# Turning gathered rows of x in 32 by 32 squares on VectorE, from four part rows per token

## The chip, the core and the metric

The kernel runs on one core of one Trainium2 chip. The metric is the device time of one execution in microseconds. The core has TensorE (PE in the profile; PEld is its loading of weights), VectorE (DVE), ScalarE (ACT), GpSimd (POOL) and the queue engine SyncE (SP), which issues most DMAs. Each engine runs its own instructions strictly in order and waits on the others through semaphores. Three runs of the kernel before gave 692.34 to 692.62 us, with a median of 692.57 us.

## What is computed

A dilated sliding-window attention makes a token's features x (512 numbers: 8 heads of 64), and a mixture of experts with one expert per token turns them into the output. The second half is what matters here:

```python
logits = np.einsum('bsd,de->bse', x, w_gate)            # 8 x 576 tokens, 8 experts
local_gate = 1.0 / (1.0 + np.exp(-np.einsum('bsd,de->bse', x, w_local).squeeze(-1)))
for s in range(S):
    fresh_e = int(np.argmax(logits[b, s]))
    e = fresh_e if (s == 0 or local_gate[b, s] < 0.5) else prev_e
    prev_e = e
    h = np.maximum(x[b, s] @ w1[e], 0.0)                # 512 -> 1024
    out[b, s] = p[e] * (h @ w2[e])                      # 1024 -> 512, p: softmax of logits
```

All data are float32. Which tokens belong to which expert is known only on the chip, so tokens are grouped by expert there.

## The kernel before

**Attention and routing.** A loop over 32 head pairs (`for n in range(NPB + 2)`) makes scores, probabilities and values. Each finished group of two head pairs of one batch is written to a scratch tensor in DRAM by SP (`store`): `xd[0]` holds the 256 features of the plain heads of every token, `xd[1]` those of the dilated heads, whose tokens stand in another order. In the gaps of that loop, one step per call of `gap`, a list called `waiting` is worked off: it holds the routing of the four groups of two batches. After two groups `early_tokens` can name the tokens of the first two units; after all four, in the gaps of the expert stage, `late_tokens` names the rest. `tokens(late)` does it: one matrix product of `acc` (the positions of all tokens, as codes) with `chosen` gives `fp`, in which partition p and column c hold the code of the p-th token of tile c, and a few integer operations on VectorE make two row numbers from it, `tok` for `xd[0]` and `pos` for `xd[1]`.

**The expert stage** works on units. A unit is a `pair` (two tiles of 128 tokens of one expert), a `full` (one tile) or a `half` (64 tokens). Two pairs come early, units 0 and 1; 22 late units follow. Numbered from zero they are P P P F P H, then P P F P H, the same five again, P P F P, and P H at the end (P pair, F full, H half); the text calls them i0 to i21. So i3, i8, i13, i18 are full and i5, i10, i15, i21 are half. For a unit u:

- `gather(u)`: GpSimd fetches its rows by an indirect DMA, one for `tok` and one for `pos` per tile, 1 KB per row, into `xg` (two buffers).
- `features(u)`: TensorE turns each tile's 128x512 into four 128x128 blocks in a PSUM bank `tp` (L820), ScalarE copies them to `xe` (L821). For a pair, four VectorE operations then make the sums `xc` (L787 to L790).
- `hidden(u)`: the first layer. For a pair it is Strassen's scheme in Winograd's form (`chain`): seven products over quarters of the matrices, with sums of the weights (`sums[0]`, four VectorE operations of 128x1024) and of the features (`xc`). Three PSUM banks x, y, z take them in turn; the first, third, fifth and seventh product go into x. `keep` copies a product away on ScalarE, `finish` adds to it on VectorE (L910).
- `output(u)`: the second layer, the same with seven products and the sums `hc` of the hidden values and `sums[1]` of the weights; `finish` writes `y` on VectorE (L984), and `send` scatters `y` to the output from GpSimd, one indirect DMA per tile. A full ends with one VectorE operation on `y` (L960).

The loop over late units is the order in which TensorE and VectorE get their work, since for these two engines the order is that of the program:

```python
for u in range(FIRST, NU):
    run_hidden(u, both(u - 1) if u > FIRST else [])   # both: hc sums and sums[1] of unit u-1, on VectorE
    if u + 1 < NU:
        features(u + 1)
        if u + 2 < NU:
            gather(u + 2)
    push = sums_of_weights(u + 1, False) if is_pair(u + 1) else []   # sums[0] of unit u+1
    if u > FIRST:
        run_output(u - 1, push)
```

The sums that are pushed are spread over the gaps between products, and what is left is issued at the unit's end. GpSimd's, ScalarE's and SP's orders are made by a scheduler. For the first late unit, i0, `features` is called in the middle of the output of unit 1 (`feed`), and i0's hidden layer is followed at once by i1's, with no output between them.

## Time and profile before

| what | value |
|---|---|
| median of 3 runs | 692.57 us |
| the profiled execution | 695.8 us, its span 693.9 us |
| granted TensorE clock, mean | 0.981 |
| busy: PE, PEld, DVE, ACT, POOL | 95%, 84%, 58%, 28%, 27% |
| DMA | 131.40 MB, mean 189 GB/s |
| attention stage | to about 170 us |
| expert stage with early units | 170 to 233 us |
| late units | 233 to 680 us, then the last scatters |

A row of the table of groups gives line, engine, operation, what it writes and reads, how often, the busy time and the mean time of one. A row of the timeline gives the start in us, the time from the start of the first to the end of the last instruction that it merges, the engine, the line and the number of instructions; what stands in square brackets is the idle time of the engine before it and what ended it. A float32 product shows as two instructions, a TensorE transpose as one. Since matmuls overlap, the time that one takes from TensorE is read from start to start of neighbouring rows, not from its own length.

### The profile page before, as it was taken

To read this page: it belongs to the slowest core of one execution; us is meant where nothing else is said; L and a number is where in the kernel's file an instruction comes from. 1 tells how busy PE (TensorE), PEld (TensorE's weight loads), DVE (VectorE), ACT (ScalarE), POOL (GpSimd) and SP (SyncE) were. 2 spreads that over 40 slices of the span, in tenths; PEclk is the share of its full clock that TensorE was granted. 3 is DMA by queue.
4 is the path that set the end of the run, shared out by engine and by line. 5 is a ranking of instruction groups with operands and counts; after the bars stand their busy time and mean duration, and the time that the engine had idled before them with its cause. 6 is when DMAs were issued, how large, how long until landed. Compare 5 with 4: busy or idle time off the path is not lost. (4 is left out here: it accounts for less than half of the span.)

```text
span 693.9 us, 14608 instructions
## 1 busy us (share of the span) xinstructions
PE 661.4 (95%) x6102; PEld 581.9 (84%) x6102; DVE 401.2 (58%) x784; ACT 191.8 (28%) x350; POOL 184.0 (27%) x181
## 2 busy tenths in 40 slices
PE   8999898898998989999999999999999999999994
PEld 8878787786987989999599999599998799997973
DVE  3758697678767377363456472637451828446450
ACT  3544343342311232312223222123222132122310
POOL 4332212311012233122453141413241423041011
PEclk9999998998999999999999999999999999999998
DMA  9999776874502677565453414744113556451201
GB/s 351 409 376 329 265 245 227 275 277 129 215 30 83 236 317 298 224 220 224 146 198 137 153 54 152 278 177 156 31 40 123 210 184 247 145 194 30 113 32 42
DMA packets 27835, 131.40 MB, mean 189 GB/s; under 512 B 3981, under 2 KB 14349, under 8 KB 21744
## 3 DMA queue, kind: packets, MB, share of 16 engines
q1 hardware_dynamic: 20912, 110.97, 43.4%
q0 software_dynamic: 6848, 19.41, 7.9%
q8 instruction: 50, 0.82, 0.5%
q14 instruction: 25, 0.20, 0.1%
HBM read 145.04 MB, written 19.40 MB: 237 GB/s over the span
## 5 line engine op out<-in xcount | busy, mean ns | idle before, releaser
L928 POOL DMA_INDIRECT out_dram<-y,tok x36 | 49.7, 1380 | 250.8 <-DVE y L984 130.2
L969 PE MATMUL yp<-sum,hc 128*128 128x256 f32 x384 | 88.2, 379 | 0.0
L900 PE MATMUL hp<-xc,sum 128*128 128x128 f32 x720 | 85.6, 275 | 1.2 <-DVE sum L781 1.2
L910 DVE TENSOR_TENSOR h<-hp,h 128x512 f32<-128x512 f32 x45 | 30.9, 689 | 95.6 <-PE hp L900 95.3
L900 PEld LDWEIGHTS hp<-xc,sum 128*128 128x128 f32 x720 | 82.9, 192 | 1.4 <-DVE sum L781 1.4
L808 POOL DMA_INDIRECT xg<-xd,tok x40 | 47.1, 1178 | 131.2 <-PE tp L820 109.5
L969 PEld LDWEIGHTS yp<-sum,hc 128*128 128x128 f32 x384 | 72.8, 190 | 9.9
L984 DVE SCALAR_TENSOR_TENSOR y<-yp,gate,y 128x256 f32<-128x256 f32 x48 | 23.2, 482 | 69.2 <-issue 44.9
L317 ACT ACTIVATE pr<-pr 96x512 f32<-96x512 f32 x64 | 43.8, 684 | 67.3 <-DVE pr L314 64.3
L308 PE MATMUL sc<-kq 64*96 64x64 f32 x1152 | 56.5, 249 | 4.9 <-DVE pr L314 3.8
L314 DVE SCALAR_TENSOR_TENSOR pr<-sc,mk 96x512 f32<-96x512 f32 x64 | 46.8, 748 | 24.8 <-PE sc L308 22.6
L969 PE MATMUL yp<-raw,h 128*128 128x256 f32 x256 | 60.7, 380 | 0.0
L257 POOL COPY vt<-vt 32x585 f32<-32x585 f32 x48 | 33.9, 707 | 100.3 <-DMA vt<-in_v_dram 65.8
L308 PEld LDWEIGHTS sc<-kq 64*96 64x96 f32 x1152 | 52.2, 163 | 9.2 <-DVE pr L314 4.2
L900 PE MATMUL hp<-xe,raw 128*128 128x128 f32 x480 | 59.0, 276 | 0.3 <-ACT xe L821 0.3
L900 PEld LDWEIGHTS hp<-xe,raw 128*128 128x128 f32 x480 | 56.5, 192 | 2.9 <-issue 2.1
L969 PEld LDWEIGHTS yp<-raw,h 128*128 128x128 f32 x256 | 47.4, 190 | 6.7 <-issue 0.8
L362 PE MATMUL pv<-vt,pr 128*64 128x65 f32 x1152 | 44.6, 230 | 5.5 <-issue 5.0
L904 ACT COPY h<-hp 128x512 f32<-128x512 f32 x45 | 26.4, 586 | 77.6 <-PE hp L900 77.6
L362 PEld LDWEIGHTS pv<-vt,pr 128*64 128x64 f32 x1152 | 39.1, 143 | 9.7 <-issue 7.0
L808 POOL DMA_INDIRECT xg<-xd,pos x40 | 43.2, 1080 | 12.2 <-issue 12.2
L911 ACT ACTIVATE h<-h 128x512 f32<-128x512 f32 x45 | 28.3, 630 | 65.1 <-DVE h L910 63.5
(209 smaller groups left out, 990.3 us busy)
## 6 DMA issues: line engine op xcount, KB each, us to landing
raw<-in_w_dram SPq DMA_DIRECT2D x48, 2048.0 KB
kq<-in_qk_dram SPq DMA_DIRECT2D x15, 1184.0 KB
vt<-in_v_dram SPq DMA_DIRECT2D x15, 880.0 KB
xd<-x SPq DMA_DIRECT2D x16, 512.0 KB
kq<-in_qk_dram SPq DMA_DIRECT2D x2, 592.0 KB
xd<-x SPq DMA_DIRECT2D x32, 32.0 KB
xg<-xd,tok POOLq DMA_INDIRECT x40
xg<-xd,pos POOLq DMA_INDIRECT x40
```

The lines of the kernel that those rows point to most:

```text
L257: nc.gpsimd.tensor_copy(t[k * WIN:(k + 1) * WIN, VQ:], t[KW:, k * NB * VW:(k + 1) * NB * VW])
L308: nc.tensor.matmul(sc[:KW, u, (i - a) * QB:(i - a + 1) * QB], lhsT=kt[h, i * QB:i * QB + KW], rhs=qt[h, i * QB:(i + 1) * QB], start=True, ...
L314: nc.vector.scalar_tensor_tensor(to, sc[:KW, :, :w], -CEIL, mk[:, at:at + w].unsqueeze(1).to_broadcast([KW, 2, w]), Alu.max, Alu.min)
L317: nc.scalar.activation(to, to, Act.Exp, scale=SCALE)
L362: nc.tensor.matmul(pv[half * QB:(half + 1) * QB, k - a], lhsT=pr[:, u, (i - a) * QB:(i - a + 1) * QB], rhs=vt[:, u, i], start=True, stop=T ...
L808: nc.gpsimd.indirect_dma_start(out=x[:rows, g], out_offset=None, in_=xd[g] if units[u]["late"] else xd[g][:EARLY * GS], in_offset=bass.Ind ...
L900: nc.tensor.matmul(to[:, m], lhsT=a[:, m, kk], rhs=b[:, kk], start=first and m == 0 and kk == 0, stop=(kk == DK // 2 - 1), skip_group_chec ...
L904: nc.scalar.copy(at((0, 1, 3)[k]), of)
L910: nc.vector.tensor_tensor(at(k), of, at(k), op=Alu.add)
L911: nc.scalar.activation(at(k), at(k), Act.Relu)
L928: nc.gpsimd.indirect_dma_start(out=out, out_offset=bass.IndirectOffsetOnAxis(ap=of_unit(u, "tok", j), axis=0), in_=y, in_offset=None, boun ...
L969: nc.tensor.matmul(to, lhsT=a[:, m], rhs=b[:, m], start=first and m == 0, stop=(m == FK // 2 - 1), skip_group_check=True)
```

## The change

The scratch tensor becomes one tensor `xd` of [token][2][256], and is read as rows of 128 features (`xq`), four to a token. One indirect DMA now fetches, for 32 tokens, their four part rows of 512 bytes into four blocks of 32 partitions, so a tile of 128 tokens takes four of them (a half two) instead of two of 1 KB rows. VectorE then turns the tile in one operation in 32 by 32 squares, from `xg` straight to `xe`; TensorE's transposes and ScalarE's copies of the features are gone. The order of the features within a block of 128 is different, and the weights w1 are laid out to match on the host.

For the row numbers, `tokens` makes a second product `fq`: for each of the four groups of 32 tokens in a tile (`square`) four small products put the tokens' codes into the four blocks of partitions, 16 products for the early units and 32 for the late ones. Six VectorE operations over four times as many columns make the row numbers `at`; two operations that made `pos` are gone.

Gathers are called one unit further ahead, with four buffers for late units. `early_tokens` puts the second half of unit 0's gathers one step further down the list `waiting`, so every later step of that list comes one gap later.

```diff
-    xd = [dram.tile([N + 1, D // 2], F32, name=f"xd{g}") for g in range(2)]
+    xd = dram.tile([N + 1, 2, D // 2], F32, name="xd")
+    xq = xd.rearrange("n g (u f) -> (n g u) f", u=2)
...
         fp = bank([P, 2, cols], "fp")
+        fq = bank([P, NQS, cols], "fq")
         chosen = tiles["chosen", late]
+
+        def square(q, at, cols, first, flags):
+
+            for part in range(NQS):
+                nc.tensor.matmul(fq[part * SQ:(part + 1) * SQ, q, cols], lhsT=acc[:, at + q * SQ:at + (q + 1) * SQ],
+                                 rhs=of[:2 * ES, 0, cols], start=first, tile_position=(0, part * SQ), **flags)
+
...
+            if late:
+                nc.vector.tensor_copy(acc[:, P:], acc[:, ROW:P])
+            for q in range(NQS):
+                square(q, 0, slice(0, w), k == 0 and q == 0, flags)
+            if late:
+                for q in range(NQS):
+                    square(q, ROW, slice(C_HALF, cols), False, flags)
             nc.tensor.matmul(fp[:, :, :w], lhsT=acc[:, :P], rhs=of[:2 * ES, :, :w], start=(k == 0), **flags)
...
+        nc.vector.tensor_scalar(codes, fq, float(NONE), None, Alu.add)
+        nc.vector.tensor_scalar(high, codes, 8, None, Alu.logical_shift_right)
+        nc.vector.tensor_scalar(at, codes, 10, None, Alu.logical_shift_right)
+        nc.vector.tensor_scalar(high, high, a_high, a_part, Alu.mult, Alu.add)
+        nc.vector.scalar_tensor_tensor(high, at, a_batch, high, Alu.mult, Alu.add)
+        nc.vector.scalar_tensor_tensor(at, codes, a_code, high, Alu.mult, Alu.add)
...
-        nc.vector.scalar_tensor_tensor(base, c, float(CI - 1), base, Alu.mult, Alu.add)
-        nc.vector.tensor_tensor(pos, base, j, op=Alu.add)
...
-    def gather(u):
-        assert not xg
-        for j in range(2 if units[u]["kind"] == "pair" else 1):
-            rows = ROW if units[u]["kind"] == "half" else P
-            xg[u, j] = x = mw.tile([P, 2, D // 2], F32, name="xg")
-            for g, what in enumerate(("tok", "pos")):
+    def gather(u, only=None):
+
+        col, late = units[u]["col"], units[u]["late"]
+        for j, n in enumerate(tiles_of(u)):
+            if only not in (None, j):
+                continue
+            xg[u, j] = x = stage.tile([P, NQS, P], F32, name="xg", bufs=4) if late else mw.tile(
+                [P, NQS, P], F32, name="xg")
+            for q in range(n):
                 nc.gpsimd.indirect_dma_start(
-                    out=x[:rows, g], out_offset=None, in_=xd[g] if units[u]["late"] else xd[g][:EARLY * GS],
-                    in_offset=bass.IndirectOffsetOnAxis(ap=of_unit(u, what, j, rows), axis=0))
+                    out=x[:, q], out_offset=None, in_=xq if late else xq[:EARLY * GS * NQS],
+                    in_offset=bass.IndirectOffsetOnAxis(ap=tiles["at", late][:, q, col + j:col + j + 1], axis=0))
 
     def features(u):
-        kind = units[u]["kind"]
-        rows = ROW if kind == "half" else P
         xe[u] = mw.tile([P, DK, 2 * P], F32, name="xe")
-        for j in range(2 if kind == "pair" else 1):
-            x = xg.pop((u, j)).rearrange("p g f -> p (g f)")
-            tp = bank([P, DK, P], "tp")
-            for kk in range(DK):
-                nc.tensor.transpose(tp[:, kk, :rows], x[:rows, kk * P:(kk + 1) * P], ident[:rows, :rows])
-            nc.scalar.copy(xe[u][:, :, j * P:j * P + rows], tp[:, :, :rows])
+        for j, n in enumerate(tiles_of(u)):
+            x = xg.pop((u, j))[:, :n].rearrange("p q (k d) -> p k q d", k=DK)
+            nc.vector.transpose(xe[u][:, :, j * P:j * P + n * SQ].rearrange("p k (q t) -> p k q t", q=n), x)
...
     def early_tokens():
         tokens(False)
-        gather(0)
+        gather(0, 0)
+        waiting.insert(0, lambda: gather(0, 1))
 
     def late_tokens():
         tokens(True)
-        wanted.append(FIRST)
-        gather_wanted()
+        gather(FIRST)
+        gather(FIRST + 1)
...
         features(FIRST)
-        gather(FIRST + 1)
+        gather(FIRST + 2)
...
         if u + 1 < NU:
             features(u + 1)
-            if u + 2 < NU:
-                gather(u + 2)
+            if u + 3 < NU:
+                gather(u + 3)
```

**VectorE, the stretch from the end of a full's output to the output of the pair before the half.** Here `xe` and `xc` are those of the pair after a half (i6, i11, i16), `hc` and the first `sum` belong to the pair before it, and the second `sum` is `sums[0]` of the pair after it. Before, and with the change:

```order
L960 TENSOR_SCALAR y<-yp,gate_2902 128x512
L781 TENSOR_TENSOR hc<-h 128x512
...
L790 TENSOR_TENSOR sum_2536<-raw_0_79,sum_2536 128x1024
L787 TENSOR_TENSOR xc<-xe 128x256
...
L783 TENSOR_TENSOR sum_80<-raw_1_2531 128x1024
L984 SCALAR_TENSOR_TENSOR y<-yp,gate_2902,y 128x256
L784 TENSOR_TENSOR sum_80<-raw_1_2531,sum_80 128x1024
L984 SCALAR_TENSOR_TENSOR y<-yp,gate_2902,y 128x256 x2
```

```order
L856 STREAM_TRANSPOSE xe<-xg 128x4x64
L995 TENSOR_SCALAR y<-yp,gate_2954 128x512
L818 TENSOR_TENSOR hc<-h 128x512
...
L827 TENSOR_TENSOR sum_2555<-raw_0_78,sum_2555 128x1024
L856 STREAM_TRANSPOSE xe<-xg 128x4x128 x2
L824 TENSOR_TENSOR xc<-xe 128x256
...
L820 TENSOR_TENSOR sum_79<-raw_1_2550 128x1024
L1019 SCALAR_TENSOR_TENSOR y<-yp,gate_2954,y 128x256
L821 TENSOR_TENSOR sum_79<-raw_1_2550,sum_79 128x1024
L1019 SCALAR_TENSOR_TENSOR y<-yp,gate_2954,y 128x256 x2
```

Two transposes stand between the sums and `xc`, ahead of the two operations on `y` that release the banks; the half's own transpose stands ahead of the full's last operation.

**TensorE at the late tokens**, in the hidden layer of unit 1 (the products into `hp`). Before, and with the change:

```order
L665 MATMUL ep<-chosen_late,cst 1x48
L889 MATMUL hp<-xe,raw_1_2531 128x256 x4
L682 MATMUL fp<-chosen_late,acc 128x2x40
L685 MATMUL fp<-chosen_late,acc 128x2x8
L889 MATMUL hp<-xe,raw_1_2531 128x256 x8
L969 MATMUL yp<-raw_1_2537,h 128x256 x4
```

```order
L674 MATMUL ep<-chosen_late,cst 1x48
L924 MATMUL hp<-xe,raw_1_2550 128x256 x4
L688 MATMUL fq<-chosen_late,acc 32x40 x16
L688 MATMUL fq<-chosen_late,acc 32x8 x16
L706 MATMUL fp<-chosen_late,acc 128x2x40
L708 MATMUL fp<-chosen_late,acc 128x2x8
L924 MATMUL hp<-xe,raw_1_2550 128x256 x4
L1004 MATMUL yp<-raw_1_2556,h 128x256 x4
```

The 32 small products stand ahead of the two old ones, and four products of the hidden layer instead of eight are left behind them: the step comes one gap later.

**GpSimd from the first late gathers on** (`at_2934` are the late row numbers, `tok_2030` are the early units' and `tok_2947` the late ones' rows of the output). With the change:

```order
L848 DMA xg<-xd,at_2934 128x128 x24
L963 DMA out_dram<-y,tok_2030 4608x512 x2
L848 DMA xg<-xd,at_2934 128x128 x14
L963 DMA out_dram<-y,tok_2947 4608x512 x2
L848 DMA xg<-xd,at_2934 128x128 x4
```

The gathers of i0, i1 and i2 (24) stand ahead of unit 1's two scatters; before, it was the eight of i0 and i1.

48 lines of the change are left out of this document (30 added, 18 removed).

## The prediction

> **What bounds the kernel now.** I read the page's busy shares first, then who TensorE waited for, then the timeline around each `features`.
>
> ```profile
> PE 661.4 (95%) x6102; PEld 581.9 (84%) x6102; DVE 401.2 (58%) x784; ACT 191.8 (28%) x350; POOL 184.0 (27%) x181
> ```
>
> ```profile
> PE pv L362 <- issue: 5.0, 8, 1.1
> ...
> PE hp L900 <- DVE sum L781: 1.2, 1, 1.2
> ```
>
> Columns of the second view: total wait in us, times, longest. TensorE is busy 95% of the span, and its longest kind of wait (5.0 us in all) lies in attention. In the expert stage little stands in that view beside one wait of 1.2 us, at i1. So an instruction taken from TensorE there is worth its time, unless another engine is just behind. Whether VectorE is, tells this view:
>
> ```profile
> DVE xc L787 <- ACT xe L821: 27.7, 11, 3.0
> ```
>
> Of the 15 pairs with `xc` sums, VectorE stood idle at 11, waiting for TensorE's transposes and the copy. At the four others it came from a backlog: unit 0 (in attention), i6, i11 and i16, the pairs after a half that follow a full's output.
>
> **What is removed.** The timeline on TensorE at a full, a pair and a half:
>
> ```profile
> 387.55 0.60 PE L820 MATMUL tp<-cst,xg 128*128 128x128 f32 x4
> 387.98 1.89 PE L969 MATMUL yp<-raw,h 128*128 128x256 f32 x8
> ...
> 407.22 1.04 PE L820 MATMUL tp<-cst,xg 128*128 128x128 f32 x8
> 408.09 1.89 PE L969 MATMUL yp<-raw,h 128*128 128x256 f32 x8
> ...
> 432.78 0.46 PE L820 MATMUL tp<-cst,xg 64*128 64x64 f32 x4
> 433.17 7.13 PE L957 MATMUL yp<-raw,h 128*128 128x512 f32 x16
> ```
>
> From start to start: 0.43 us for a full, 0.87 for a pair, 0.39 for a half. At the places without backlog that is gained: nine late pairs (i2, i4, i7, i9, i12, i14, i17, i19, i20) 7.8, four fulls 1.7, four halves 1.6, unit 1 and i0 1.7 (what i0's gathers do is a term below): 12.8 us. ScalarE's copies go too; at 28% busy they bound nothing.
>
> **What VectorE gets: the three pairs after halves.** No transpose on VectorE stands in this trace. The stretch at i6, where VectorE works off the sums of i4 behind the last operation of the full i3:
>
> ```profile
> 340.60 0.75 DVE L960 TENSOR_SCALAR y<-yp,gate 128x512 f32<-128x512 f32 x1 [8.55 <-PE yp L957]
> ...
> 341.58 0.67 DVE L781 TENSOR_TENSOR hc<-h 128x512 f32<-128x512 f32 x1
> 342.18 1.21 DVE L787 TENSOR_TENSOR sum<-raw 128x1024 f32<-128x1024 f32 x1
> ...
> 348.53 0.41 DVE L787 TENSOR_TENSOR xc<-xe 128x256 f32<-128x256 f32 x1
> ...
> 353.76 1.89 PE L969 MATMUL yp<-raw,hc 128*128 128x256 f32 x8
> 355.07 0.47 DVE L984 SCALAR_TENSOR_TENSOR y<-yp,gate,y 128x256 f32<-128x256 f32 x1
> 355.59 1.99 PE L969 MATMUL yp<-sum,h 128*128 128x256 f32 x8
> ```
>
> VectorE has no gap from 340.60 on. Its second operation on `y` ends at 355.07 + 0.47 = 355.54, and TensorE's seventh product, which adds into the same bank, starts at 355.59: it could have started at 355.49 (sixth product 1.73 long). So VectorE sets the end here already, by 0.1 us. Two transposes ahead of `xc` push the seventh product back by two of their times, and the 0.87 us that TensorE saves is waited away. Price of one: the nearest row is the 128x512 sum, 341.58 to 342.18, 0.60 us. Below, an element as fast as in a one-input operation (300 ns for 288, so 0.53):
>
> ```profile
> L1081 DVE TENSOR_SCALAR y<-rec 128x288 f32<-128x288 f32 x1 | 0.3, 300 | 0.0
> ```
>
> Above, two cycles an element, as the 1.21 us of 128x1024. I take 0.60, since the transpose too reads and writes 512 elements a partition in SBUF. Less a slack of up to 0.1, that is +1.15 at each of i6, i11, i16: +3.4 us.
>
> The Trainium skill (VectorE: DVE Perf Modes, The three transpose paths and Rules for kernel authors) speaks against the change: it sends a 128x128 transpose to TensorE if PSUM may receive it, and gives 311 ns on VectorE against 390 on TensorE for bf16. The rows above have TensorE at 0.11 us each in a run of eight, so the page's 390 isn't what is gained here. Its 311 ns would make a tile 178 + 533 = 711 ns, an estimate; with that for the 0.60 the time is 0.7 us longer.
>
> **i1**, which follows i0 with no output between:
>
> ```profile
> 244.38 0.69 DVE L910 TENSOR_TENSOR h<-hp,h 128x512 f32<-128x512 f32 x1 [1.02 <-PE hp L900]
> 245.97 1.04 PE L820 MATMUL tp<-cst,xg 128*128 128x128 f32 x8
> ...
> 247.76 0.43 DVE L787 TENSOR_TENSOR xc<-xe 128x256 f32<-128x256 f32 x1 [2.69 <-ACT xe L821]
> 249.24 1.22 DVE L781 TENSOR_TENSOR sum<-raw 128x1024 f32<-128x1024 f32 x1
> ...
> 250.51 3.84 PE L900 MATMUL hp<-xc,sum 128*128 128x128 f32 x32 [1.16 <-DVE sum L781]
> ```
>
> The second product waits for that sum. With the change VectorE needn't wait for TensorE's transposes: two of 0.60 from 245.07, `xc` 1.48, the sum 1.27 with its hand-over: 249.0 instead of 250.5, a gain of 1.5 us.
>
> **Unit 0** lies at 153 us in attention, before a stretch where VectorE is full (the window below, 9.49 of 10 us): TensorE -0.9, VectorE +1.2. I take 0, bounds -0.9 and +1.2.
>
> **The new products** (`square`): 16 early, 32 late, two instructions each, so 32 and 64 on TensorE, with 32 columns of weights and 4 to 40 of data.
>
> ```profile
> L362 PE MATMUL pv<-vt,pr 128*64 128x65 f32 x1152 | 44.6, 230 | 5.5 <-issue 5.0
> ```
>
> ```profile
> 216.60 0.35 PE L682 MATMUL fp<-chosen_late,acc 112*128 112x80 f32 x2
> 216.78 0.33 PE L685 MATMUL fp<-chosen_late,acc 112*128 112x16 f32 x2
> 216.96 3.70 PE L889 MATMUL hp<-xe,raw 128*128 128x256 f32 x16
> 217.15 0.21 DVE L690 TENSOR_SCALAR code<-fp 128x48 int32<-128x48 f32 x1 [1.06 <-PE fp L685]
> ...
> 218.53 0.21 DVE L697 CUSTOM_DVE_ANT_0 pos<-base,j 128x96 uint16<-128x96 uint16 x1
> 219.03 0.99 POOL L808 DMA_INDIRECT xg<-xd,tok  x1 [12.84 <-DVE side L703]
> ...
> 222.23 3.62 PE L969 MATMUL yp<-sum,hc 128*128 128x256 f32 x16
> ...
> 223.15 1.04 POOL L808 DMA_INDIRECT xg<-xd,pos  x1 [0.30 <-issue]
> ...
> 229.13 1.04 PE L820 MATMUL tp<-cst,xg 128*128 128x128 f32 x8
> ...
> 235.25 3.74 PE L900 MATMUL hp<-xc,sum 128*128 128x128 f32 x32
> ```
>
> L362, also small and in column groups: 44.6 us / 1152 = 39 ns each. The four old instructions took 0.36 us, 90 ns each. I take 39, the nearer shape: 1.25 + 2.5 = +3.75 us on TensorE (1.9 if more column groups overlap further, 8.6 at 90 ns).
>
> **The late gathers.** The step comes one gap later, 8 of the 16 instructions of 216.96: 1.85 us; the squares 2.5; six operations of 192 columns (about 0.3 each by L1081) against eight of 0.2: +0.2. So the first gather moves from 219.03 to 223.6. GpSimd takes (223.15 - 219.03) / 3 = 1.4 us from issue to issue at most, 1.27 as a rule (0.95 to 1.0 and 0.3 between); the eight of i0 are out by 233.8. The last of before was out at 224.2 and needed at 229.13 without a wait, so landing takes up to 4.9: 238.7. One transpose and the first `xc`, 1.0, give 239.7 for the second product of i0, which would start at 235.25 - 0.87 + 2.5 = 236.9. Behind the waiting transpose stand unit 1's last `y` and a sum, which nobody needs earlier. Wait 0 to 2.8; I take 1.4. Also the `hc` sums of unit 1 stand behind 14 index operations, which end at 221.5 + 1.8 + 1.6 = 224.9; the first sum at 225.6, where the second product of its output is due at 222.23 + 2.5 = 224.7: +0.9. Together +2.3.
>
> Sum: -12.8 + 3.4 - 1.5 + 3.75 + 2.3 = -4.85 us. The profiled execution's 695.8 would become 691.0; it lies 3.2 above the median, and the same difference makes 692.57 into **687.7 us**.
>
> **Rivals.** For three of them:
>
> ```profile
> 133.22 1.04 POOL L808 DMA_INDIRECT xg<-xd,tok  x1 [3.10 <-issue]
> ...
> 137.62 0.37 PE L362 MATMUL pv<-vt,pr 128*64 128x65 f32 x4 [0.99 <-issue]
> ```
>
> ```profile
> 160.00:170.00 10.00, 8.02 (x88) 5.80 (x91) 9.49 (x27) 3.38 (x7) 0.00 (x0) 0.68 0.19 60
> ```
>
> ```profile
> 448.03 1.17 POOL L808 DMA_INDIRECT xg<-xd,tok  x1 [0.30 <-issue]
> ...
> 449.50 1.96 POOL L808 DMA_INDIRECT xg<-xd,pos  x1 [0.30 <-issue]
> ```
>
> ```profile
> POOL out_dram L928 <- DMA out_dram<-y,tok: 51.6, 10, 8.1
> ```
>
> - Nothing binds after the halves and the squares overlap: -12.8 - 3 x 0.87 - 1.5 + 1.9 + 0.9 = -14: 678.5, or half-way, 683. For it, VectorE is busy 58% overall. Against it, 355.54 and 355.59. Chance 0.15.
> - A transpose takes 1.2 us: + 3 x 1.2 at the halves, 1.2 at i1, 1.2 at unit 0: 693.7, no change. Nothing in the trace speaks for it or against it. Chance 0.13.
> - Attention's stalls grow: the 5.0 us of TensorE's "issue" waits (at 137.62 among others) fall where early gathers run (from 133.22). If they go with the number of gathers, +5: 692.7, no change. But the bytes stay, and stores move there too. Chance 0.10.
> - **Slower: GpSimd gets slow at i0.** It has 24 gathers before unit 1's scatters. At 1.27 us each it keeps up: in five units P P F P H it has 30 gathers, 38 us, 8 scatters, 10 at the same price, and three waits of at most 8.1 for a first scatter to land: 72 of some 100 us (22 late units take 447). But single issues take 1.96 us (449.50). At 1.75 a gather, i0's eight are out at 237.6, their second tile is turned at 243.5, and the wait is 6.6 instead of 1.4; i1 waits some 2.5 more: 695.5. It decides from about 1.65 us a gather. Chance 0.17. The Trainium skill (SBUF — State Buffer, SBUF: two separate sides) has a reason for it: GpSimd can't write a DMA's descriptors while VectorE holds the shared ports in a two-port mode. The 1.96 us row fits, but its neighbour of 1.17, beside sums of the same kind, shows that it isn't the rule here.
>
> **How the numbers follow.** The forecast has 0.45, with a range of its own of 684 to 691. With the first rival (0.15) and the part of the others that ends below, faster by over 0.2% (1.4 us, about what a measurement of this kernel can tell from no change) has 0.63; within 0.2%, the second and third, 0.20; slower 0.17. The range goes from 681.5 (squares at 1.9, no waits at i0, unit 0 gained: -9, and some of the first rival) to 695 (a transpose of 1.2 us, or slow gathers).
>
> **What would show it.** No L820; the row of VectorE's transposes near 0.6 to 0.7 us; TensorE going from hidden to output with no gap; a wait of about 2 us for `y` before the seventh product at i6, i11, i16, and none at the other pairs; the small products taking some 2.5 us at the late tokens; a wait of TensorE on `xc` at i0 of 0 to 3 us; gathers of 1.27 us from issue to issue. The forecast is wrong if VectorE's transposes take far from 0.6 us, if TensorE waits on gathers, or if attention's end moves by more than 2 us.

## The result, and the profile after

Four runs of the change gave 715.23 to 721.13 us with a median of 719.95 us, beside 692.34 to 698.23 us for four of the kernel before. The ratio is 1.036, with an interval of 1.029 to 1.043: slower, by 25 us (27 by the medians) where 4.85 us less were forecast. In every ratio of this text, executions more than 1.5% above the fastest of the same kernel are left out. The profiled execution took 721.13 us, its span is 719.3 us. The page has TensorE doing less work than before (657.7 us busy against 661.4) in a longer span, and the clock at 0.6 in the fifteenth of 40 slices of 18 us, from 252 us on:

```profile
PE 657.7 (91%) x6038; PEld 573.5 (80%) x6038; DVE 427.7 (59%) x832; ACT 172.3 (24%) x310; POOL 261.0 (36%) x253
...
PEclk9799899887999968999999999999999999999998
```

The stages are read from the timeline, by the starts of TensorE's first products: "attention" ends with unit 0's first hidden product, "early" with i0's first, "i0 and i1" with the first output product after them, "late" with the last unit's first output product. In us:

| execution | attention | early | i0 and i1 | late | span |
|---|---|---|---|---|---|
| before | 170.6 | 62.9 | 29.7 | 404.9 | 693.9 |
| the change | 182.5 | 62.1 | 48.8 | 399.8 | 719.3 |
| difference | +11.9 | -0.8 | +19.1 | -5.1 | +25.4 (tail +0.3) |

So the long part of the kernel gained, as forecast, and two short places, where gathers run one behind the other, lost 31 us. Both show in the view of waits with a word that stands in the trace of before too and that the prediction does not weigh, "remote": the signal that released the engine came with no recorded instruction ending near it.

```profile
ACT h L939 <- remote: 22.8, 2, 16.3
DVE h L945 <- remote: 15.9, 1, 15.9
PE hp L935 <- issue: 9.3, 5, 5.9
ACT xt L394 <- remote: 9.0, 1, 9.0
DVE xe L856 <- DMA xg<-xd,at: 8.4, 1, 8.4
PE hp L935 <- ACT h L939: 6.7, 1, 6.7
PE yp L1004 <- DVE y L1019: 6.1, 4, 2.1
```

**i0, the timeline** (TensorE's products, the transposes, and those who wait for products):

```profile
243.62 0.94 POOL L848 DMA_INDIRECT xg<-xd,at  x1 [0.30 <-issue]
...
244.55 1.95 PE L935 MATMUL hp<-xe,raw 128*128 128x128 f32 x16
246.73 0.58 ACT L939 COPY h<-hp 128x512 f32<-128x512 f32 x1 [1.50 <-PE hp L935]
...
251.13 0.71 DVE L856 STREAM_TRANSPOSE xe<-xg 128x512 f32<-128x512 f32 x1 [8.39 <-DMA xg<-xd,at]
...
252.36 6.27 PE L935 MATMUL hp<-xc,sum 128*128 128x128 f32 x32 [5.86 <-issue]
...
258.46 1.50 PE L935 MATMUL hp<-xe,raw 128*128 128x128 f32 x12
...
260.12 0.27 PE L935 MATMUL hp<-xe,raw 128*128 128x128 f32 x1 [0.16 <-issue]
...
260.84 0.36 PE L935 MATMUL hp<-xe,raw 128*128 128x128 f32 x1 [0.45 <-issue]
...
262.92 0.27 PE L935 MATMUL hp<-xe,raw 128*128 128x128 f32 x1 [1.72 <-issue]
...
263.63 0.58 ACT L939 COPY h<-hp 128x512 f32<-128x512 f32 x1 [16.32 <-remote]
264.32 0.37 PE L935 MATMUL hp<-xe,raw 128*128 128x128 f32 x1 [1.13 <-issue]
...
270.72 0.58 ACT L939 COPY h<-hp 128x512 f32<-128x512 f32 x1 [6.50 <-remote]
270.95 0.69 DVE L945 TENSOR_TENSOR h<-hp,h 128x512 f32<-128x512 f32 x1 [15.94 <-remote]
271.36 3.56 PE L935 MATMUL hp<-xc,sum 128*128 128x128 f32 x16 [6.67 <-ACT h L939]
```

The first product ends at 246.50 (244.55 + 1.95), and ScalarE's copy of it starts 0.23 us later: so fast is the hand-over as a rule. The second and third product end by 258.63 (252.36 + 6.27), the fourth at 264.69 (264.32 + 0.37). Their readers start at 263.63, 270.72 and 270.95: 5.0 (at least), 12.1 and 6.3 us late. The last two start 0.23 us apart although a product lies between them: the word that they are done arrived late, for two of them at once. The fifth product needs the bank that the copy at 270.72 empties, and everything stands. In this trace the fourth product is slow as well: its last four instructions start at 260.12, 260.84, 262.92 and 264.32, with 3.5 us of idle time that ends with "issue", that is, without a wait that the profile shows. A second trace of the change, from chip 0 (its run stands below), has the late word without that; the same four places there:

```profile
248.66 5.67 PE L935 MATMUL hp<-xc,sum 128*128 128x128 f32 x32 [5.78 <-issue]
...
254.16 1.95 PE L935 MATMUL hp<-xe,raw 128*128 128x128 f32 x16
264.27 0.59 ACT L939 COPY h<-hp 128x512 f32<-128x512 f32 x1 [9.96 <-remote]
...
265.87 0.69 DVE L945 TENSOR_TENSOR h<-hp,h 128x512 f32<-128x512 f32 x1 [14.61 <-remote]
```

The third product ends by 254.33 and the fourth, which takes the usual 1.95 us, at 256.11; their readers start 9.9 and 9.8 us later. The ends of products are modelled by the profile, so that a late signal can't be told from a late end behind it. The text calls it a late signal of TensorE.

The +19.1 splits so: the second tile's rows come late, and TensorE waits 5.86 us; after that wait two products take 6.27 us where the row quoted of before has 3.74, with the clock that the windows below show, +2.5; and the fourth product, begun at 258.46, would have ended by 260.4 if it took 1.95 us as the first, but the fifth starts at 271.36, 11 us later. The rest of the stretch is even. The windows, whose columns are busy time and instructions of TensorE, its weight loads, VectorE, ScalarE and GpSimd, then the granted clock, the share of DMA and GB/s:

```profile
247.00:249.00 2.00, 0.00 (x0) 0.00 (x0) 0.00 (x0) 0.31 (x1) 1.39 (x3) 1.00 1.00 426
...
250.00:270.00 20.00, 8.87 (x48) 8.09 (x48) 3.81 (x7) 0.58 (x1) 13.26 (x14) 0.69 0.23 70
```

**Attention** shows the same around unit 0's eight gathers. The first and the last of them, TensorE's first unexplained stop, and the transpose that waits for ScalarE, which waits 9.0 us "remote" for TensorE's transposes:

```profile
134.78 1.03 POOL L848 DMA_INDIRECT xg<-xd,at  x1 [3.36 <-issue]
...
143.64 0.94 POOL L848 DMA_INDIRECT xg<-xd,at  x1 [0.30 <-issue]
```

```profile
135.21 2.34 PE L317 MATMUL sc<-kq 64*96 64x64 f32 x26 [1.96 <-issue]
...
147.00 0.47 PE L390 MATMUL tp<-cst,x 128*128 128x128 f32 x1 [4.90 <-ACT xt L394]
```

TensorE's busy time in the stretch from 130 to 150 is 12.82 of 20 us, where the kernel before has 17.27. Over the whole stage, the +11.9 us are 7.4 us more of idle time (26.0 against 18.6) and 4.5 us more of busy time (156.5 against 152.0), with the clock granted at 0.89 in the stage where it was 0.94 before. But the kernel before isn't free of late signals either; in its attention stage stands

```profile
DVE rec L366 <- remote: 5.0, 1, 5.0
...
DVE pr L314 <- remote: 1.7, 1, 1.7
```

with four gathers of 1 KB rows in place of eight of 512 bytes.

### The profile page after: what moved, and what is told of

The parts are those of the page before. It is cut to its first block, busy times and chain, and to the rows that moved or that the text cites. A ratio compares the mean times of both kernels' runs of the same rounds, so it can differ in the third digit from the quotient of the medians.

```text
span 719.3 us, 14589 instructions
## 1 busy us (share of the span) xinstructions
PE 657.7 (91%) x6038; PEld 573.5 (80%) x6038; DVE 427.7 (59%) x832; ACT 172.3 (24%) x310; POOL 261.0 (36%) x253
## 5 line engine op out<-in xcount | busy, mean ns | idle before, releaser
L848 POOL DMA_INDIRECT xg<-xd,at x152 | 165.8, 1091 | 156.7 <-DVE xe L856 97.8
L935 PE MATMUL hp<-xc,sum 128*128 128x128 f32 x720 | 90.0, 283 | 13.8 <-ACT h L939 6.7
L935 PEld LDWEIGHTS hp<-xc,sum 128*128 128x128 f32 x720 | 86.9, 200 | 15.3 <-ACT h L939 7.8
L317 PE MATMUL sc<-kq 64*96 64x64 f32 x1152 | 59.9, 257 | 8.2 <-DVE pr L323 3.9
L317 PEld LDWEIGHTS sc<-kq 64*96 64x96 f32 x1152 | 55.3, 170 | 12.9 <-issue 7.0
L1004 PE MATMUL yp<-sum,h 128*128 128x256 f32 x128 | 32.2, 397 | 6.1 <-DVE y L1019 6.1
```

Source lines behind the costliest of these rows:

```text
L317: nc.tensor.matmul(sc[:KW, u, (i - a) * QB:(i - a + 1) * QB], lhsT=kt[h, i * QB:i * QB + KW], rhs=qt[h, i * QB:(i + 1) * QB], start=True, ...
L848: nc.gpsimd.indirect_dma_start(out=x[:, q], out_offset=None, in_=xq if late else xq[:EARLY * GS * NQS], in_offset=bass.IndirectOffsetOnAxi ...
L935: nc.tensor.matmul(to[:, m], lhsT=a[:, m, kk], rhs=b[:, kk], start=first and m == 0 and kk == 0, stop=(kk == DK // 2 - 1), skip_group_chec ...
L1004: nc.tensor.matmul(to, lhsT=a[:, m], rhs=b[:, m], start=first and m == 0, stop=(m == FK // 2 - 1), skip_group_check=True)
```

## Experiments

The theory after the result: TensorE's signals are held back while many small gathers follow each other, with three versions of what counts (the length of the run of gathers, the descriptors in flight, the number and size of rows). The main rival: it is something else that the change does there, such as the longer list of steps or VectorE's transposes. Times of kernels are compared only on one chip; that turned out to matter.

**First, on chip 0**, where one run of the kernel before gave 703.68 us. Gathers called one unit later, to shorten the run:

```diff
     def late_tokens():
         tokens(True)
         gather(FIRST)
-        gather(FIRST + 1)
```

> The changed kernel with late gathers called as far ahead as before the change: i0's at the late tokens, i1's in the middle of unit 1's output, every other unit's two units ahead (8 gathers in a run at most, where the change has 24 in a run at i0). Theory 1 (TensorE's results are held back as long as GpSimd issues a long unbroken run of gathers): the stretch from i0's first product to the first product of the output, 48.8 us with the change and 29.7 before, falls to 31 to 36 us, the time to 702 to 708 us; attention stays 9 to 12 us longer than before. Theory 2 (every gather costs the other engines the same, wherever it stands): the stretch stays above 43 us, the time at 715 to 721 us. Theory 3 (the stretch is long only since VectorE waits for the rows to land): VectorE's wait of 8.4 us at i0 falls below 3 us and the stretch by 6 to 9 us, the time to 710 to 714 us.

717.93 us; attention 180.8, i0 and i1 47.4. GpSimd had no pause: still 22 gathers stood in a row, from 231 to 261, where the change has 24. So the edit hardly shortened the run, and says nothing on its length.

Two gathers of whole 1 KB rows for a tile, at the token's row numbers:

```diff
-            for q in range(n):
+            for g in range(n // 2):
                 nc.gpsimd.indirect_dma_start(
-                    out=x[:, q], ... in_=xq ..., ap=tiles["at", late][:, q, col + j:col + j + 1]
+                    out=x[:, 2 * g:2 * g + 2].rearrange("p q f -> p (q f)"), ... in_=xr ..., ap=of_unit(u, "tok", j)
```

> The changed kernel, but each tile is gathered by two DMAs of 1 KB rows instead of four of 512 bytes (the same bytes; the rows are those of other tokens, so the output is not the reference's); VectorE's transposes, the new products, the row numbers and the one gap of delay all stay. Theory 1 (long runs of gathers) and theory 2 (the number of gathers): unit 0's run has 4 gathers and i0's 12, attention ends within 4 us of where it ended before (170.6 us), the stretch from i0's first product to the first product of the output falls from 48.8 to 30 to 40 us, the time to 690 to 704 us. If instead the delayed list, the transposes or the new products cost the time, attention still ends at 180 to 183 us and the time stays at 712 to 721 us.

687.83 us; attention 168.6, i0 and i1 29.8, late 399.5. No wait of this kernel is "remote". TensorE's longest waits in the expert stage are the 6.1 us for `y` after the halves and one of 2.0 us for ScalarE at i0. Everything else of the change is in this kernel: VectorE's transposes, the squares, the longer list. So none of these by itself makes the 27 us that lie between it and the change on this chip (715.3, in a run below).

Half the room for descriptors:

```diff
-    nc = _bacc.Bacc(..., dynamic_dma_scratch_size=2048)
+    nc = _bacc.Bacc(..., dynamic_dma_scratch_size=1024)
```

> The changed kernel with half the room for the descriptors of GpSimd's DMAs (1024 instead of 2048 bytes a partition). If GpSimd's gathers fill that room and hold the other engines back as long as it is full, the stalls come earlier in each run and grow: a gather takes more than 1.25 us from issue to issue in i0's run, the time 725 us or more. If the room does not matter, 715 to 721 us and 1.25 us from issue to issue as with the change.

714.75 us, attention 180.2, i0 and i1 44.5; most gathers still follow each other at 1.25 us. Half the room changes nothing.

The other way round, the kernel before, with TensorE's transposes, and only its gathers split in two of 512 bytes a row:

```diff
-                nc.gpsimd.indirect_dma_start(out=x[:rows, g], ... in_=xd[g] ...)
+                rows_of = xd[g].rearrange("n (u f) -> (n u) f", u=2)
+                for f in (slice(0, P), slice(P, 2 * P)):
+                    nc.gpsimd.indirect_dma_start(out=x[:rows, g, f], ... in_=rows_of ...)
```

> The kernel before, with each of its gathers split into two of 512 bytes a row (twice as many gathers, the same bytes; rows of other tokens, so the output is not the reference's); TensorE's transposes, the order and the number of units ahead all stay as before. Theory 2 (the number of gathers): attention ends 7 to 12 us later than before and the time is 700 to 712 us. Theory 1 (long unbroken runs): unit 0's run has 8 gathers as with the change, so attention ends 7 to 12 us later, but the late units keep their pace (runs of 8), 699 to 706 us. If the stalls come from other parts of the change (the delayed list, VectorE's transposes, rows of one tensor), 692 to 696 us.

717.22 us; attention 178.3, i0 and i1 38.4, and its waits have the word:

```profile
DVE rec L366 <- remote: 13.4, 3, 9.9
ACT xt L385 <- remote: 12.8, 2, 6.9
ACT h L906 <- remote: 7.8, 3, 6.7
```

On this chip the late signals come with 512-byte gathers, in the old kernel as in the new, and go without them. This is the pair that carries the explanation. It is one run of each kernel, with a difference of 27 and of 24 us to the other kind of rows (the kernel before took 693.43 there, the median of seven). It doesn't tell the number of gathers from the size of the rows, since both kernels change the two together.

**Then, on chip 11** (before: 689.80 in one run), to tell those apart and to slow the gathers down. Four gathers of 64 rows of 1 KB, so that the number stays and the rows are as few as before; the list not delayed; and GpSimd copying the row numbers before each gather, six times in the first such kernel and once in the second, with three gathers in flight at most:

```diff
-            for q in range(n):
-                nc.gpsimd.indirect_dma_start(out=x[:, q], ... in_=xq ...)
+            for g in range(n // 2):
+                for r in (0, ROW):
+                    nc.gpsimd.indirect_dma_start(out=x[r:r + ROW, 2 * g:2 * g + 2]..., in_=xr ...)
```

> The changed kernel with four gathers per tile, each of 64 rows of 1 KB instead of 128 rows of 512 bytes (as many DMAs and as many bytes as the change, half as many rows; rows of other tokens, so the output is not the reference's). If the number of DMAs that GpSimd issues decides: 712 to 721 us, attention ends at 179 to 183 us. If the number of rows (and so of descriptors) decides: 687 to 696 us, attention ends at 168 to 174 us, as with two gathers of 128 rows of 1 KB (687.8 us).

```diff
-        gather(0, 0)
-        waiting.insert(0, lambda: gather(0, 1))
+        gather(0)
```

> The changed kernel with unit 0's eight gathers called in one step, as before, so that no step of the list comes a gap later. If the delay of the list by one gap costs part of attention's 12 us, attention ends 2 us or more earlier than with the change (182.5) and the late tokens 3 us earlier or more; if the gathers alone cost it, 715 to 721 us and less than 2 us at attention's end.

```diff
+                own = once.tile([P, 16], I32, name="own_row", bufs=3)
+                for _ in range(6):
+                    nc.gpsimd.tensor_copy(own, row.to_broadcast([P, 16]))
                 nc.gpsimd.indirect_dma_start(..., ap=own[:, :1] ...)
```

> The changed kernel with a pause ahead of each gather: GpSimd copies the gather's row numbers six times (128x16) into one of three small tiles, so that gathers no longer stand back to back and no more than three are on their way. Theory 1 (a long unbroken run of gathers holds TensorE's results back): attention ends within 5 us of where it ended before (170.6), and no result of TensorE comes more than 2 us after its product; the late rows come later instead, the time is 692 to 708 us. Theory 2 (every gather costs the same wherever it stands): 715 to 721 us. If the landing of i0's rows is what costs most, the pause makes that wait longer than the 8.4 us of the change, and the time is over 721 us.

> As the run with pauses, with one copy instead of six: hardly a pause, but still no more than three gathers on their way at a time. If it is the number of gathers on their way that holds TensorE up, the stalls go and the time is 690 to 705 us; if it is GpSimd's issuing back to back, the stalls stay in part and it lies between the change and the run with six copies.

Measured: 685.87 with 64 rows (attention 165.5, i0 and i1 27.6), 692.99 without the delay (172.6 and 27.6), 845.73 and 714.86 with the copies. In none of the four is there a "remote" wait of TensorE's readers. I read the second of these as the answer (the delayed list makes the difference), too early, as the next runs showed: the change itself hadn't run on this chip. The paced kernels show what pacing costs: GpSimd waits for its own gathers to land, in the one with one copy for 53.7 us between 300 and 700 us.

**On chip 15** (before: median 691.77 of 13), the kernel without the delay again, with its times; the delay alone, as an edit of the kernel before; 1 KB rows for the early units alone; and an edit at the waits for `y`, on top of the kernel without the delay, which issues the weight sums behind the operations on `y` where a half follows:

> The same kernel as the run without the delayed list (unit 0's eight gathers called in one step), timed against the kernel before. If the 693 us of the first run is what this kernel does, all runs lie at 689 to 697 us, 22 us or more under the change; if it was a chance outcome of one run, some lie at 710 us or more.

689.63 (ten runs of 686.13 to 692.43), a ratio of 0.998, 0.994 to 1.002.

```diff
-        gather(0)
+        gather(0, 0)
+        waiting.insert(0, lambda: gather(0, 1))
```

> The kernel before with only one edit: the gathers of unit 0's second tile are put one step further down the list, as in the change, so every later step comes a gap later (gathers stay at 1 KB a row). If the delay by itself costs what its removal gave (27 us), attention ends 4 us or more after the kernel before (170.6) and the time is 697 us or more. If it costs only together with twice as many rows, attention ends within 2 us and the late tokens come one gap (about 2 us) later: 690 to 696 us.

691.21, attention 164.0, i0 and i1 29.7. In the kernel before the delay by itself costs nothing. Nor has this kernel, which is else the kernel before, a "remote" wait on this chip: the 5.0 and 1.7 us in the trace of before may mark the chip that it was taken on.

```diff
-            for q in range(n):
+            for g in range(0 if late else n // 2):
+                nc.gpsimd.indirect_dma_start(... in_=xr[:EARLY * GS * 2] ...)
+            for q in range(n if late else 0):
                 nc.gpsimd.indirect_dma_start(...)
```

> The changed kernel (delayed list and all), but with the early units' tiles gathered by two DMAs of 1 KB rows (rows of other tokens, so the output is not the reference's); late units are gathered as in the change. If the stall at i0 belongs to the late gathers of 512 bytes themselves, attention ends at 167 to 174 us and the stretch from i0's first product to the first product of the output stays at 44 to 49 us: 702 to 712 us. If it only comes where work happens to fall together, as the run without the delayed list suggests, it may go too: 687 to 696 us.

695.5, attention 168.2, i0 and i1 36.0. No "remote" here at i0 either, where the gathers are those of the change; what is left there is a wait of VectorE of 8.2 us for rows. On a chip without late signals this kernel cannot tell what it was made to tell.

```diff
         if u > FIRST:
-            run_output(u - 1, push)
+            half = units[u]["kind"] == "half"
+            run_output(u - 1, [] if half else push)
+            if half:
+                now(push)
```

> As the run without the delayed list, and at the three pairs after a half (i6, i11, i16) the sums of the weights for that pair's first layer are issued behind the output's operations on y instead of between them. By the prediction's step on VectorE TensorE waits 2 us for y at each of these places only since two sums and two transposes stand ahead of it: the waits of TensorE on y (5.9 us in three) go and the time falls by 5 to 7 us against the run without the delayed list, to 684 to 690 us. If VectorE is just as late at the next place (the second product of the pair's first layer waits for the sum), the time stays within 2 us.

678.92 (677.4 to 680.99), a ratio of 0.983, 0.977 to 0.990. The waits for `y` are gone, and the late stage is 391.1 us, 13.8 below the kernel before.

**On chip 7** (before: median 687.83, 13 runs of 685.1 to 692.54), the change itself at last, beside the kernel without the delay, the split kernel, and the change with the edit at the halves:

> The changed kernel itself, once more and on the same chip as the runs beside it. If TensorE's signals come late in it whatever the chip (as in all four runs so far and in the two kernels next to it, 715 to 721 us), it takes 712 to 722 us here too, beside 686 to 693 for the kernel without the delayed list. If the chip was the cause, it takes 692 to 702 us here.

The median of ten runs is 694.77 (684.26 to 698.47). The ratio is 0.998, 0.993 to 1.003; by the medians of all runs it is 1.010. So on this chip the change is even to 1% slower, and no wait is "remote". The profiled execution (689.95 us): attention 163.8, early 62.1, i0 and i1 35.5, late 401.2. Of the waits above these are left:

```profile
DVE xe L856 <- DMA xg<-xd,at: 8.4, 1, 8.4
PE yp L1004 <- DVE y L1019: 6.1, 4, 2.1
```

> The kernel without the delayed list, on the same chip as the change: 686 to 694 us with no late signal of TensorE if the order of the list decides; 710 us or more if the chip does.

691.62, attention 173.2, i0 and i1 27.5. The delayed list alone doesn't make signals late: the change has it and they are not late here. This took back my reading of chip 11.

> The kernel before with twice as many gathers of half the size, once more (717.2 us where the kernel before took 703.7 on the chip of that run). If the rows of 512 bytes by themselves make TensorE's signals late, 705 to 720 us and waits of ScalarE and VectorE that no recorded work ends; if that was the chip, 690 to 700 us.

695.42, attention 166.6, i0 and i1 31.9, and no "remote". The same kernel took 717.22 on chip 0.

> The changed kernel, delayed list and all, with the sums of the weights behind the operations on y at the three pairs after a half. The waits of TensorE on y (6.1 us in four) go: 5 to 9 us under the change on the same chip. The late signals in attention and at i0 are not touched by this edit, so where the change shows them, this kernel does too.

677.46, attention 166.4, early 65.1, i0 and i1 27.5, late 391.1. The rows of i0 are in time here; the next section shows what goes with that.

**Chip 0 again** (before: median 693.43, seven runs of 691.62 to 694.66, so the 703.68 of the first run was not typical; it has no trace, so whether signals were late in it, with rows of 1 KB, is not known), with the change and the edited change:

> The changed kernel a third time, to see on a further chip whether TensorE's signals come late. Without late signals: 684 to 699 us, as on the chip before, attention ending at 163 to 174 us. With them: 712 to 722 us, attention ending after 178 us.

715.3; attention 178.8, i0 and i1 46.7, late 399.9, with the waits of the first result: "remote" are 14.6 us of VectorE and 10.0 of ScalarE at i0, and 9.8 of ScalarE in attention.

> The changed kernel with the sums of the weights behind the operations on y at the three pairs after a half, timed. Without late signals of TensorE on this chip: 675 to 683 us, a ratio of 0.975 to 0.99 to the kernel before. With late signals it loses what the change loses: 705 to 715 us.

709.91 (706.82 to 710.86), a ratio of 1.023, 1.019 to 1.027; attention 182.3, i0 and i1 45.3, late 392.7.

So one kernel takes 677 us on chip 7 and 710 on chip 0, and the change is even on one and 22 us slower on the other. Which chip the first comparison ran on isn't known; by its waits it is one like chip 0.

## Why the prediction was wrong

**The step that failed first: what the gathers do to the engines that wait for TensorE.** The sum had nothing for it: unit 0's term, 0 with bounds of -0.9 and +1.2, weighed only the engines' own work, and i0 had a term for its rows alone. The third rival, "attention's stalls grow", had +5 us in attention and a chance of 0.10, and nothing at i0. It costs 11.9 us in attention and some 11 at i0. The 11.9 hold some us by which attention's end moves without any late signal: it lies at 163.8 to 173.2 in seven profiled executions with 512-byte gathers throughout, unpaced, on chips 7, 11 and 15, with the granted clock of the stage at 0.96 in the earliest and 0.91 in the latest. The rival also named other waits than those that grew. TensorE's "issue" waits at the row that it priced went from 5.0 to 0.7 us:

```profile
L371 PE MATMUL pv<-vt,pr 128*64 128x65 f32 x1152 | 44.3, 235 | 0.8 <-issue 0.7
```

What grew are the "remote" waits of those who read TensorE's products, from 6.7 to 12.7 us in attention and from none to 38.7 at i0; the nearest sign of them ahead of the change was VectorE's "remote" wait of 5.0 us in the trace of before, which is not those 5.0 us of TensorE. The prediction gave "the bytes stay" as the reason against the rival. The pair on chip 0 contradicts that: with the same bytes, 1 KB rows give 687.83 and no late signal, and 512-byte rows in the old kernel give 717.22 with them. Two of the prediction's own signs of being wrong came: attention's end moved by more than 2 us, and TensorE waited on gathers.

What stays open: why a signal of TensorE is late at all, why TensorE's own instructions come slowly beside it in some of these traces, why on chip 0 and not on 7, 11 and 15, and whether it is the number of gathers, of rows, or the length of the run; the kernel with 64 rows, which could tell the first two apart, ran on a chip that doesn't show it. It is not shown either that one chip always does so: chip 0 did in five of the five kernels with 512-byte gathers that ran there.

**The second step: i0's rows, wait 0 to 2.8.** It is 8.4 us for VectorE and 5.86 for TensorE in the recorded profile, and 8.4 and 5.74 on chip 7, where signals are in time: this part doesn't come from late signals. Two sizes of the sum were too small. The eight gathers of i0 were taken at 1.27 us from issue to issue; later ones do follow at 1.25 (0.94 each and 0.30 between), but these take 1.53 on average (232.93 to 243.62), two of them 1.38 and 2.01 us long. It is the direction of the last rival, slow issues, short of its 1.75. So the last of them ends at 244.56, as i0's first product starts (244.55), where the sum had it 1.3 us ahead of that (233.8, and 235.1 for the product). And their rows take 6.6 us to land, where the sum had at most 4.9. The 1.3 and the 1.7 are the 3 us by which the wait passes its bound of 2.8.

When rows land late shows the last gather of i0's second tile beside SP's load of 2 MB of weights that is issued at about the same time, in three profiles; first the change, whose gather and transpose stand in the timeline above at 243.62 and 251.13:

```profile
243.02 0.34 SPq L782 DMA_DIRECT2D raw<-in_w_dram  x1
```

The change on chip 7:

```profile
225.00 0.94 POOL L848 DMA_INDIRECT xg<-xd,at  x1 [0.30 <-issue]
...
232.39 0.71 DVE L856 STREAM_TRANSPOSE xe<-xg 128x512 f32<-128x512 f32 x1 [8.35 <-DMA xg<-xd,at]
...
233.62 5.88 PE L935 MATMUL hp<-xc,sum 128*128 128x128 f32 x32 [5.74 <-DVE xc L824]
```

```profile
224.40 0.34 SPq L782 DMA_DIRECT2D raw<-in_w_dram  x1
```

And the edited change on chip 7:

```profile
227.61 1.39 POOL L848 DMA_INDIRECT xg<-xd,at  x1 [0.30 <-issue]
...
230.69 0.71 DVE L856 STREAM_TRANSPOSE xe<-xg 128x512 f32<-128x512 f32 x1 [0.97 <-DMA xg<-xd,at]
```

```profile
229.95 0.34 SPq L782 DMA_DIRECT2D raw<-in_w_dram  x1
```

Where the gather ends before the load is issued (229.00, 229.95), its rows are there 1.7 us later. Where it ends after (244.56 and 243.02; 225.94 and 224.40), they are there 6.6 and 6.5 us later, with DMA at 1.00 and 426 GB/s in between. All twelve traces with unpaced late gathers of 512 bytes into the changed layout fall into these two groups: in seven the gather ends 1.5 to 1.6 us behind the load's issue and the rows take 6.4 to 6.6 us, in five it ends 0.9 to 1.0 us ahead of it and they take 1.6 to 1.8. The four kernels without the delayed list are all among the five; of the eight traces with it only the edited change on chip 7 is, and the same kernel on chip 0 is among the seven. So with the change's gathers the delay goes with late rows, though it costs nothing in the kernel before. That the load is the cause is read from these coincidences and wasn't tried by moving the load alone. The prediction took landing as "up to 4.9" from the first late gathers of the kernel before. DMA moved 412 to 416 GB/s there too, from 224 to 228 us, so the number was a bound from when those rows were needed, and no price of standing behind a load. The stage of i0 and i1 is 27.5 us where rows are in time and 35.5 where they are not, with 29.7 before.

**What was right.** The late units gain: predicted -11.1 + 3.4 = -7.7, measured -5.1 and, on chip 7, -3.7. The wait before the seventh product of the output after a half was foreseen at i6, i11 and i16 and is there, three times 2 us (the fourth of the view is 0.2 at another place). At the first two of the three halves the loss is the predicted one: TensorE's time from the output's first product to the next hidden's goes from 12.7 to 15.0 and from 12.5 to 14.8, that before it from 4.5 to 3.6 both times: +1.3 each, for 1.15 predicted. At the third it is +3.0 (12.5 to 16.5, and 4.6 to 3.6). The timeline of TensorE at the three seventh products:

```profile
385.15 1.99 PE L1004 MATMUL yp<-sum,h 128*128 128x256 f32 x8 [2.08 <-DVE y L1019]
...
483.14 1.99 PE L1004 MATMUL yp<-sum,h 128*128 128x256 f32 x8 [1.90 <-DVE y L1019]
...
581.45 3.53 PE L1004 MATMUL yp<-sum,h 128*128 128x256 f32 x8 [1.90 <-DVE y L1019]
```

Behind the third wait the seventh product takes 3.53 us instead of 1.99, and the granted clock in the windows (the column behind the busy times) is 0.66:

```profile
581.00:586.00 5.00, 4.55 (x18) 3.77 (x19) 0.79 (x3) 0.87 (x2) 3.73 (x4) 0.66 0.89 367
```

So a wait of 1.9 us can cost as much again behind it. The Trainium skill (TensorE: Matmul & The Clock Gate, Part 1: The HAM clock gate) puts the change to half rate after an idle window of about 3.4 us; here it came after 1.9 us, and after 2.08 and 1.90 us at the two other places it did not. On chip 7 it came behind two of the three waits (2.09 and 1.91 us; the seventh products take 3.15 and 2.83 us) and not behind the one of 1.90, and the late stage is over 1 us longer than in the first trace.

The first rival, nothing binds after the halves, was right about the size of the gain without that wait: -11.1 and three times -0.87 are -13.7, and the edited order, in which it doesn't occur, has -13.8 (391.1 against 404.9). What it had wrong was that the change reaches it by itself.

**Sizes.** Transposes, taken as 0.60 us, and gathers:

```profile
L848 POOL DMA_INDIRECT xg<-xd,at x152 | 165.8, 1091 | 156.7 <-DVE xe L856 97.8 <-issue 42.7 <-DVE base L733 15.0
L856 DVE STREAM_TRANSPOSE xe<-xg 128x512 f32<-128x512 f32 x36 | 23.6, 687 | 8.6 <-DMA xg<-xd,at 8.4 <-issue 0.2
...
L856 DVE STREAM_TRANSPOSE xe<-xg 128x256 f32<-128x256 f32 x4 | 1.7, 435 | 0.0
```

0.687 us is near the 711 ns that the prediction worked out from the Trainium skill (VectorE: DVE Perf Modes, The three transpose paths and Rules for kernel authors) in a sentence of its own; the second rival, 1.2 us, is false. The squares, taken as 1.25 and 2.5 us:

```profile
131.85 0.43 PE L688 MATMUL fq<-chosen_early,acc 112*32 112x4 f32 x32
132.21 0.39 PE L706 MATMUL fp<-chosen_early,acc 112*128 112x8 f32 x2
```

```profile
229.31 0.77 PE L688 MATMUL fq<-chosen_late,acc 112*32 112x40 f32 x64
230.01 0.45 PE L706 MATMUL fp<-chosen_late,acc 112*128 112x80 f32 x2
```

0.36 and 0.70 us from start to start, 11 ns an instruction: the lower bound of 1.9 was still too high. The early stage, predicted at +1.7 (2.5 + 0.9 - 1.7), is -0.8. For i1 the prediction had -1.5; with rows in time the stage of i0 and i1 is 2.2 shorter (27.5 against 29.7).

**The sum, where no signal is late**, is thus -0.8 in the early stage, +5.8 for i0 and i1 and -3.7 in the late stage on chip 7, against the stages of the trace of before: +1.3, which is no change, as chip 7 has it. No trace has the change itself with its rows in time. In the five traces where they are, the early stage is longer, 62.3 to 65.1 us, and with i0 and i1 it takes 89.8 to 92.6, against 97.6 for the change on chip 7 and 92.7 before; with the late stage's -3.7 that would be a sum of -3.8 to -6.5. That the forecast of -4.85 lies in there is luck: its late stage gains 4 us too much and its squares cost 2.7 us too much. Whether the last gather ends ahead of the load of weights or behind its issue, which is what goes with rows in time or late, is in none of its terms.

**The better version.** The change with the weight sums behind the `y` operations after a half takes 677.46 us on chip 7, 10.4 below the kernel before in one run, and without the delayed list 678.92 on chip 15, 0.983 of before. On chip 0 it is slower than the kernel before, 1.023. Whole rows of 1 KB gave 687.83 there, but that kernel doesn't have the layout that VectorE's 32 by 32 transposes need. So no version is shown to beat the kernel before on every chip: the first of the two loses on chip 0, and the second ran on chip 15 alone.

## What to carry to other kernels

A wait in the trace of before that no instruction explains can be a price that a change multiplies: ask what runs beside it, what the change does to the number of those, and whether another chip shows it. Before naming the cause of a large difference, run the change itself and the kernel before on a second chip; an experiment on another chip than the result's can look like a cure when there was nothing to cure. Small gathers that are needed soon are better issued ahead of a bulk load of weights (here 0.95 us ahead was enough), and an operation that TensorE's next product waits for belongs ahead of sums that nobody needs yet.

## What the runs showed of the hardware

- On chip 0, readers of TensorE's products started 9.8 and 9.9 us after the products' recorded ends (0.23 as a rule) in a trace of the change with gathers of 512-byte rows. In the first comparison, on a chip not known, it was 5.0 to 12.1 us, and the readers of two products, with a whole product between, started 0.23 us apart. On chips 7, 11 and 15 no trace with such gathers has it. The same kernel took 717.22 us on chip 0 and 695.42 on chip 7, another 709.91 and 677.46.
- Gathers of 128 rows are mostly 1.25 us apart from issue to issue, with 512-byte rows as with 1 KB rows; what differs between the two is their number for a tile. Single ones took 1.3 to 2.0 us.
- In seven traces a gather whose issue ended 1.5 to 1.6 us behind the issue of a 2 MB load had its rows 6.4 to 6.6 us later; in five, one that ended 0.9 to 1.0 us ahead of it 1.6 to 1.8 us later.
- The granted clock fell to half (0.50 from 582 to 585 us) after a wait of 1.9 us in one place of a trace and not after 1.90 and 2.08 us in two others; on chip 7 it fell behind two such waits of three.
